# A DeltaNet and GELU kernel: chunk 0's masked Gram products taken from the plain Gram matrix, another home for chunk 2's Gram matrix, and a new order of the early work

## The chip, the cores and the metric

The kernel runs on one core of a Trainium2 chip. The metric is device time in microseconds; the median of several runs is compared. Beside the runs there is one profiled execution, whose trace shows every instruction on the engines PE (matrix unit; its weight loads are PEld), DVE (vector), ACT (scalar), POOL (GpSimd) and SP (here only a queue for DMA issues). ACT and POOL can issue DMAs too.

## The reference

Each of 4 x 8 heads runs a delta rule over 768 steps with a 48 x 48 state; the results, 3072 tokens of 384 numbers, go through a GELU network of width 2048.

```python
k_n = k / (np.linalg.norm(k, axis=-1, keepdims=True) + 1e-06)
state = np.zeros((B, H, D, D), dtype=np.float32)
for t in range(S):
    kt, vt, bt = (k_n[:, :, t].copy(), v[:, :, t].copy(), beta[:, :, t, None].copy())
    y[:, :, t] = np.einsum('bhd,bhde->bhe', q[:, :, t], state)
    v_old = np.einsum('bhde,bhd->bhe', state, kt)
    state = state + bt[:, :, :, None] * np.einsum('bhd,bhe->bhde', kt, vt - v_old)
x = y.transpose(0, 2, 1, 3).reshape(B * S, H * D)
h = x @ w_in
out = 0.5 * h * (1.0 + np.tanh(c * (h + 0.044715 * h * h * h))) @ w_out
```

## The kernel before

The sequence is cut into 12 chunks of 64 steps. A chunk c has two units, u = 2c and 2c + 1, each with 16 of the 32 heads; two heads share the 128 partitions. Within a chunk the delta rule is solved by the inverse of a triangular 64 x 64 matrix per head, built from 8 x 8 leaves upward; then the state is carried on and the chunk's 256 tokens go through the network. Every operation has a name with its chunk or unit behind the dot:

- Loads: k, q, v with chunk and quarter (k5.10 is a quarter of chunk 5's keys), beta, and w1, w2 (the weights, by POOL's queue). A chunk's k, q and v go to one of three buffers.
- Norms of the keys, per chunk (0a and 0b for the halves of chunk 0): sq (square), sum, pow (root), eps, inv.
- prep, per unit: kn (normalized keys), qb and vb (copies to bf16), knc, qbc, vbc (the same for both units of a chunk in one instruction); Tk, Tq or T (transposes on PE) and their copies kTk, kTq, kT; GD, GQ or G (Gram matrices of keys with keys and with queries), the copy dn of the first, wq (the second under its mask; wqa and wqb do it in two steps).
- leaf, per chunk: F gathers the leaves of dn, lp scales them, L spreads them, and x0, xm1 to xm6, xa1 to xa6 solve them step by step on DVE; xb ends it.
- scale, per unit: xe spreads xb to the block matrix zt (xec does both units at once); KZ multiplies the keys by zt, kz copies that, with the sign turned, to the third part of kT; GM forms the scaled Gram products from it (32 matmuls); lw writes them, under a mask, into the unit's lw buffer.
- invert, per unit: X10 and X11 put the leaves into the matrix bd, A4, rt4, B4, bde40 and bde41 join them to 32 x 32, A5, rt5, B5, be50 and be51 to 64 x 64.
- chain, per chunk: V, K, R (right hand side), U, Un (solution), S, Sn (new state), Q, O, On (output), X, xT (its transpose; turnx by DMA later).
- mlp, per chunk: up0 to up15 (3 matmuls each of 256 columns), gelu0 to gelu3, down00 to down13 (4 matmuls each of 384 columns), Z0, Z1, out.

Constants are made at the start (tmpl, ident, rows, blk, own, sel, unit, mlw, muq, two, low, pads, bdz, triwq, trilw, ladj). tabS and tabG are tiny activations that load ACT's tables for the square root and for the GELU. A fill is one matmul of 128 x 128 zeros by 128 x 512 zeros whose result nobody reads.

The order of all this is written out by hand in one list, ORDER (line 17 on). A word such as xe.1:d puts xe.1 on DVE (a, g, s: ACT, POOL, SP); a word with @4 is PE work that takes PSUM banks from bank 4 on. Each engine runs its words strictly in the order of the list. Flow.order (L152) finds from the list who must wait for whom, for data and for PSUM banks, and emit (L190) writes the semaphores.

## Time and profile before

| | us |
|---|---|
| median of 3 runs | 255.19 |
| the 3 runs | 253.28, 255.19, 255.27 |
| profiled execution, first to last instruction (its span; no other time of it is given) | 254.7 |
| PE busy | 226.0 (89%) |
| DVE busy | 185.8 (73%) |
| ACT busy | 157.4 (62%) |
| POOL busy | 130.1 (51%) |

A row of a timeline gives start and length in us, the engine, the line of the kernel, the operation, out<-in with the tile's names, shapes and a count; in brackets stands the idle time ahead of it and who ended it. A row of a grouping gives busy us and the mean ns of one, then the idle time ahead. Shares of busy time are averages over stages with different limits, so the windows matter more than this table.

### The profile page before, as it was taken

To read this page: it belongs to the slowest core of one execution; us is meant where nothing else is said; L and a number is where in the kernel's file an instruction comes from. 1 tells how busy PE (TensorE), PEld (TensorE's weight loads), DVE (VectorE), ACT (ScalarE), POOL (GpSimd) and SP (SyncE) were. 2 spreads that over 40 slices of the span, in tenths; PEclk is the share of its full clock that TensorE was granted. 3 is DMA by queue.
4 is the path that set the end of the run, shared out by engine and by line. 5 is a ranking of instruction groups with operands and counts; after the bars stand their busy time and mean duration, and the time that the engine had idled before them with its cause. 6 is when DMAs were issued, how large, how long until landed. Compare 5 with 4: busy or idle time off the path is not lost.

```text
span 254.7 us, 12256 instructions
## 1 busy us (share of the span) xinstructions
PE 226.0 (89%) x5500; PEld 178.3 (70%) x5502; DVE 185.8 (73%) x445; ACT 157.4 (62%) x244; POOL 130.1 (51%) x159
## 2 busy tenths in 40 slices
...
GB/s 103 165 144 118 184 162 95 165 127 117 128 130 105 112 126 124 135 165 147 119 146 167 100 36 131 147 153 130 56 93 167 62 49 4 33 68 64 3 93 62
DMA packets 104532, 28.25 MB, mean 111 GB/s; under 512 B 98592, under 2 KB 103712, under 8 KB 104480
## 3 DMA queue, kind: packets, MB, share of 16 engines
...
q8 instruction: 43, 0.70, 1.2%
q10 hardware_dynamic: 2400, 0.54, 1.1%
...
HBM read 20.64 MB, written 4.72 MB: 100 GB/s over the span
## 4 chain that ended last, share of the span: by engine, by line
PE 73%; DVE 15%; ACT 4%; DMA 2%; ACTq 2%; issue 2%; SPq 1%; POOL 0%
PE ps L835 24%; PE ps L824 22%; PE ps L692 5%; PE ps L620 3%; PE ps L752 3%; PE ps L773 2%; DMA vraw<-in_v_dram 2%; PE ps L697 2%; PE ps L564 2%; DVE lw L623 2%; DVE xl L658 2%; PE ps L633 2%; PE ps L759 2%; DVE ps L655 2%; PE ps L609 1%
## 5 line engine op out<-in xcount | busy, mean ns | idle before, releaser
L824 PE MATMUL ps<-xT,W 128*128 128x256 bf16 x576 | 76.8, 277 | 0.4 <-DVE xl L658 0.4
L835 PE MATMUL ps<-W,gT 128*128 128x384 bf16 x384 | 72.7, 326 | 0.0
L828 ACT ACTIVATE gT<-ps 128x1024 bf16<-128x1024 f32 x48 | 48.4, 1022 | 26.4 <-PE ps L824 25.8
L824 PEld LDWEIGHTS ps<-xT,W 128*128 128x128 bf16 x576 | 52.2, 99 | 9.3 <-DVE xl L658 0.5
L835 PEld LDWEIGHTS ps<-W,gT 128*128 128x128 bf16 x384 | 34.0, 97 | 18.2
L682 POOL TENSOR_SCALAR_AFFINE_SELECT bd<-lw 64x512 bf16<-64x512 bf16 x34 | 22.6, 667 | 37.7 <-DVE lw L623 28.6
L704 DVE TENSOR_TENSOR rl<-ps,two 128x384 bf16<-128x384 f32 (+1 forms) x48 | 22.9, 484 | 9.7 <-PE ps L692 9.5
L623 DVE CAST_PREDICATED lw<-mlw,ps 128x832 bf16<-128x832 uint16 x24 | 24.3, 1018 | 6.8 <-PE ps L620 6.5
L499 POOL TENSOR_TENSOR nrm<-nrm,half 128x16 f32<-128x16 f32 x9 | 26.6, 2956 | 2.8 <-DVE nrm L497 2.7
L343 ACT ACTIVATE bd<-ps 32x256 bf16<-32x256 f32 (+1 forms) x40 | 16.8, 428 | 8.2 <-PE ps L692 4.4
L692 PEld LDWEIGHTS ps<-lw,bd 128*128 128x128 bf16 x384 | 15.5, 98 | 4.2 <-POOL bd L682 1.2
L692 PE MATMUL ps<-lw,bd 128*128 128x32 bf16 (+1 forms) x384 | 17.2, 183 | 1.2 <-POOL bd L682 1.1
L658 DVE TENSOR_TENSOR xl<-ps,xl 128x96 bf16<-128x96 f32 (+4 forms) x72 | 16.0, 228 | 2.0
L655 DVE TENSOR_TENSOR ps<-ps,xl 128x64 f32<-128x64 f32 (+5 forms) x72 | 15.6, 221 | 2.0 <-PE ps L649 0.5
L343 ACT ACTIVATE ob<-ps 128x384 f32<-128x384 f32 x17 | 8.3, 490 | 14.0 <-PE ps L835 14.0
L722 POOL COPY bd<-xi 64x256 f32<-64x256 f32 x20 | 8.0, 401 | 16.4 <-ACT xi L343 8.5
L540 PE MATMUL ps<-ident,tok 128*128 128x128 bf16 x80 | 7.8, 246 | 8.1 <-POOL tok L531 3.8
L531 POOL TENSOR_TENSOR tok<-kraw,nrm 128x384 bf16<-128x384 f32 x9 | 8.5, 945 | 12.7 <-DVE bsb L349 5.6
L349 ACT ACTIVATE kT<-ps 128x512 bf16<-128x512 f32 x18 | 10.4, 596 | 6.4 <-PE ps L609 6.4
L343 ACT ACTIVATE dn<-ps 128x512 bf16<-128x512 f32 x18 | 10.4, 593 | 5.3 <-PE ps L564 5.3
L620 PE MATMUL ps<-kT 48*64 48x56 bf16 (+1 forms) x768 | 11.1, 196 | 2.8 <-ACT kT L349 1.4
L599 POOL TENSOR_TENSOR zt<-xb,blk 128x2048 bf16<-128x2048 bf16 x3 | 10.9, 3642 | 4.1 <-DVE xb L669 3.9
(132 smaller groups left out, 428.3 us busy)
## 6 DMA issues: line engine op xcount, KB each, us to landing
...
```

The lines of the kernel that those rows point to most:

```text
L343: return e.activation(out, in_, ACT.Copy) if e is nc.scalar else e.tensor_copy(out, in_)
L499: if e is nc.scalar else e.tensor_tensor(nr[:, 1, hx], nr[:, 0, hx], half[:, hx], ALU.pow), reads=[nrn, "half"] + ["one"] * (c < ROOTS),
L620: ins = e.matmul(P(ps("GM"))[hf(a), o_ + c0:o_ + c1], kT[s][r, y, g, hf(a)], kT[s][r, z, g, C * a + c0:C * a + c1])
L623: A(("dve",), op("lw"), lambda e, P: e.copy_predicated(lw[m][:, :, 0:LW - LB], mlw[:, :, :].rearrange("p w t -> p (w t)")[:, 16:16 + LW - ...
L655: A(("dve",), f"xm{m}.{c}", lambda e, P, m=m, w=w, part=part: e.tensor_tensor(part(P), P(f"L.{c}")[:, off[m]:off[m] + 2 * H * w].rearrange ...
L658: A(("dve",), f"xa{m}.{c}", lambda e, P, m=m, part=part: e.tensor_tensor(xl[y][:, :, m + 1:LB], part(P), xl[y][:, :, m + 1:LB], ALU.add), ...
L682: A(("pool", "dve"), op(f"X1{a}"), lambda e, P, src=lw[m][hf(a), :, LW - C:LW], dst=bd[b_][hf(a), :, hf(a)], a=a: e.affine_select(out=dst, ...
L692: ins = e.matmul(P(name)[:, C * h + c0:C * h + c1], bd[b_][:, h, :], rhs[:, h, :])
L704: A(("dve",), op(f"rt{i}"), lambda e, P, i=i, c0=c0, c1=c1, r_=r_: e.tensor_tensor(r_[:, 0:H, c0:c1], P(ps(f"A{i}")).rearrange("p (h t) -> ...
L824: ins = e.matmul(P(ph)[:, 256 * f:256 * f + 256].rearrange("p (x t) -> p x t", x=2), W1[:, j, 128 * (i + f):128 * (i + f) + 128], x_[:, :, ...
L828: A(("act",), f"gelu{i // 4}.{c}", lambda e, P, i=i, ph=ph: e.activation(g_[:, i:i + 4, :], P(ph).rearrange("p (f t) -> p f t", f=4), ACT. ...
L835: ins = e.matmul(P(po)[:, 0:DM], g_[:, f, 128 * b:128 * b + 128], W2[:, f, :], start=(f == 0), stop=(f == FC - 1))
```

## The change

The scaled Gram products are sums over the leaf index of entries that dn already holds: for chunk 0 GM is now formed from dn and zt directly (direct, 32 matmuls), and KZ.0, KZ.1, kz.0 and kz.1 go. The signs are kept by copying betaC0 without the minus and by putting it into R.0. dn of the even chunks stood in one buffer; chunk 2's now stands in the first quarter of gT2, a buffer that is first needed for chunk 2's GELU, and gelu0.2 waits for its readers. Loads and outputs may stand on ACT's queue too, and the count on a DMA's semaphore follows the list instead of the queues.

```diff
...
+        gram_of = [(dn[c % 2], c % 2) if c != 2 else (gT[2][:, 0:4, :].rearrange("p f (h t) -> p (f h) t", t=C), 2) for c in range(NC)]
...
-                    A(EV, f"betaC{i}", lambda e, P, i=i, d0=d0, d1=d1, w=w: neg(
+                    A(EV, f"betaC{i}", lambda e, P, i=i, d0=d0, d1=d1, w=w: (neg if i else copy)(
...
-                            A(("sp", "act") if c == 0 and n == "k" else SP, f"{n}{c}" + ("" if x is None else f"x{x}") + f".{a}{y}",
+                            A(("sp", "act"), f"{n}{c}" + ("" if x is None else f"x{x}") + f".{a}{y}",
...
-            d_, dnn = dn[c % 2][:, H * x:H * x + H, :], f"dn{c % 2}{x}"
+            d_, dnn = gram_of[c][0][:, H * x:H * x + H, :], f"dn{gram_of[c][1]}{x}"
...
-            def keys(e, P):
-                for g in range(4):
-                    for p, a in quad:
-                        ins = e.matmul(P(ps("KZ"))[hf(p), 512 * a + C * g:512 * a + C * g + C], tok[s][hf(a), 0, 2 * g + p, :], zt[m][hf(a), 4 * p + g, hf(a)])
-                return ins
-            A(PE, op("KZ"), keys, reads=[n("tok0"), f"zt{m}"], alloc=(ps("KZ"), 2), mode="t", mm=16)
-            A(EV, op("kz"), lambda e, P: neg(e, kT[s][:, 2, :, :].rearrange("p g (a t) -> p a g t", a=2), P(ps("KZ")).rearrange("p (a r) -> p a r", a=2)[:, :, 0:4 * C].rearrange("p a (g t) -> p a g t", g=4)),
-              frees=[ps("KZ")], writes=[n("kTz")])
-
...
-            A(PE, op("GM"), gram, reads=[n("kTk"), n("kTz")], alloc=(ps("GM"), 2), mode="t", mm=32)
+            def direct(e, P):
+                for g in range(4):
+                    for p in range(2):
+                        h, o_ = 4 * p + g, 512 * p + 2 * C * g
+                        for a in range(2):
+                            e.matmul(P(ps("GM"))[hf(a), o_ + LW - C:o_ + LW - LB], zt[m][hf(a), h, hf(a)], d_[hf(a), h, 0:C - LB])
+                        for a in range(2):
+                            ins = e.matmul(P(ps("GM"))[hf(a), o_:o_ + C - 16], d_[hf(a), h, :], zt[m][hf(a), h, C * a + 16:C * a + C])
+                return ins
+            if c < 1:
+                d_, dnn = gram_of[c][0][:, H * x:H * x + H, :], f"dn{gram_of[c][1]}{x}"
+                A(PE, op("GM"), direct, reads=[dnn, f"zt{m}"], alloc=(ps("GM"), 2), mode="t", mm=32)
+            else:
+                def keys(e, P):
+                    for g in range(4):
+                        for p, a in quad:
+                            ins = e.matmul(P(ps("KZ"))[hf(p), 512 * a + C * g:512 * a + C * g + C], tok[s][hf(a), 0, 2 * g + p, :], zt[m][hf(a), 4 * p + g, hf(a)])
+                    return ins
+                A(PE, op("KZ"), keys, reads=[n("tok0"), f"zt{m}"], alloc=(ps("KZ"), 2), mode="t", mm=16)
+                A(EV, op("kz"), lambda e, P: neg(e, kT[s][:, 2, :, :].rearrange("p g (a t) -> p a g t", a=2), P(ps("KZ")).rearrange("p (a r) -> p a r", a=2)[:, :, 0:4 * C].rearrange("p a (g t) -> p a g t", g=4)),
+                  frees=[ps("KZ")], writes=[n("kTz")])
+
+                A(PE, op("GM"), gram, reads=[n("kTk"), n("kTz")], alloc=(ps("GM"), 2), mode="t", mm=32)
...
-                    ins = e.matmul(P(f"F.{c}")[:, 0:2 * H * (LB - 1)], sel[:, i, :], dn[y][:, :, LB * i + 1:LB * i + LB], start=(i == 0), stop=(i == NLB - 1))
-                return ins
-            A(PE, f"F.{c}", fold, reads=["sel", f"dn{y}0", f"dn{y}1"], alloc=(f"F.{c}", 1), mode="m", mm=NLB)
+                    ins = e.matmul(P(f"F.{c}")[:, 0:2 * H * (LB - 1)], sel[:, i, :], gram_of[c][0][:, :, LB * i + 1:LB * i + LB], start=(i == 0), stop=(i == NLB - 1))
+                return ins
+            A(PE, f"F.{c}", fold, reads=["sel"] + [f"dn{gram_of[c][1]}{x}" for x in range(2)], alloc=(f"F.{c}", 1), mode="m", mm=NLB)
...
-            A(EV, op("R"), lambda e, P: copy(e, rb[:, :, :, :, :].rearrange("p y x g d -> p y (x g d)"), banks(P(ps("K")))), frees=[ps("K")], writes=[rbn])
+            A(EV, op("R"), lambda e, P: (neg if first else copy)(e, rb[:, :, :, :, :].rearrange("p y x g d -> p y (x g d)"), banks(P(ps("K")))), frees=[ps("K")], writes=[rbn])
...
-                  reads=["one"], frees=[ph], writes=[f"{gn}.{i // 4}"])
+                  reads=["one"], frees=[ph], writes=[f"{gn}.{i // 4}"] + ([f"dn2{x}" for x in range(2)] if c == 2 and not i else []))
...
-                        A(SP, f"out{a}{a}.{c}", lambda e, P, a=a, o_=o_: e.dma_start(
+                        A(("sp", "act"), f"out{a}{a}.{c}", lambda e, P, a=a, o_=o_: e.dma_start(
```

In emit, the loop that counts each operation's tag runs over self.queue instead of over the engines' queues one after the other; nothing else is changed there.

The list is rewritten up to about chunk 3's leaves and unit 11; behind that the engines' orders are the same, with other PSUM banks. These are the engines' orders of the early part, from the start to the first up-projections (words without banks).

```
before
PE: betaT1 betaT0 Tk.1 Tk.2 Tk.3 Tq.1 GD.3 Tq.0 GD.2 GD.1 betaS1 Tk.0 F.1 GQ.1 GD.0 L.1 GQ.0 F.0 betaS0 betaS3 L.0 T.5 Tq.3 T.4 betaS2 Tq.2 G.5 G.4
  KZ.1 GM.1 KZ.0 F.2 L.2 GM.0 KZ.2 KZ.3 GM.3 A4.1 A4.0 B4.1 GQ.2 GM.2 B4.0 V.0 A4.3 A5.1 GQ.3 A5.0 B4.3 B5.1 B5.0 fill115 A4.2 U.0 KZ.4 O.0 A5.3 S.0
  GM.4 X.0 B4.2 fill85 KZ.5 up4.0 up0.0 up1.0 up2.0 up12.0 up3.0 A5.2 up13.0
DVE: bdz3 bdz5 pad0 pad5 trilw0 bdz4 mmlw identf sel unit mmuq betaN101 sum.0b betaN100 eps.0b inv.0b betaN001 sum.1 betaN011 betaN110 pad3 inv.1
  triwq1 betaN010 low1 kn.2 kn.3 kTk.2 betaN111 kTk.1 kTq.1 sum.0a betaH1 eps.0a inv.0a betaN000 betaL1 betaH0 sum.2 first0 kTq.0 kTk.0 lp.1 betaL0
  x0.1 two inv.2 wz xm1.1 wq.0 xa1.1 xm2.1 xa2.1 lp.0 xm3.1 ladj5.1 ladj4.1 x0.0 xm1.0 xa1.0 xa3.1 xm2.0 xa2.0 xm4.1 xm3.0 xa3.0 xa4.1 xm5.1 xm4.0
  xa4.0 xa5.1 xm5.0 xm6.1 xa6.1 xa5.0 kTq.3 xm6.0 xa6.0 xb.0 xe.1 xe.0 wq.4 xec.1 lw.1 lp.2 bdz1 x0.2 lw.0 xm1.2 xa1.2 lw.3 rt4.1 xm2.2 xa2.2 xm3.2
  xa3.2 rt4.0 xm4.2 wq.2 lw.2 xa4.2 xm5.2 rt4.3 rt5.1 rt5.0 xa5.2 xm6.2 xa6.2 be50.1 wq.3 be51.0 xe.4 bde41.3 rt4.2 sum.3 rt5.3 xe.5 lw.4 sum.4 kz.5
  X10.4 qbc.3 rt5.2 eps.3 inv.3 knc.3 lw.5
ACT: k0x1.10 k0x1.00 beta10 k0x1.11 beta00 k0x0.00 trilw1 k0x0.10 tabS sq.0b k0x0.11 pow.0b sq.1 k0x0.01 ladj4.0 pow.1 qb.1 sq.0a kTk.3 pow.0a sq.2
  dn.3 dn.2 dn.1 pow.2 dn.0 qbc.2 betaC0 triwq2 wqa.1 kT.5 betaC1 kT.4 betaC2 kTq.2 dn.4 kz.1 dn.5 ladj5.0 wqa.5 betaC3 kz.0 kz.3 kz.2 vb.0 bde40.1
  bde41.1 bde40.0 bde41.0 R.0 bde40.3 be50.0 be51.1 sq.3 Un.0 kz.4 On.0 sq.4 Sn.0 xT.0 bde40.2 bde41.2 tabG gelu0.0 gelu3.0 gelu1.0 be51.3 be50.2
  gelu2.0 be51.2 R.1
POOL: tmplz tmpl0 tmpl1 blk1 one pad2 ident ident2 bdz0 blk2 blk3 half own triwq4 triwq0 mln0 bdz2 pad4 mwp0 rowz mln1 pad1 kn.1 muq0 muq1 eps.1 qb.0
  rows1 rpad0 kn.0 low2 eps.2 trilw2 knc.2 w1.0 first1 qb.3 trilw3 qb.2 xb.1 triwq5 w1.1 mwp1 X10.1 X11.1 rpad1 X11.0 X10.0 X11.3 vb.1 triwq3 X10.3
  wqb.1 X11.2 X10.2 xb.2 w2.0 w2.1 X11.4 pow.3 X11.5 vbc.1 pow.4 bdc40.5 bdc41.5 eps.4 wqb.5
```
```
after
PE: betaT1 betaT0 Tk.3 Tk.2 Tk.1 GD.3 GD.2 betaS1 Tq.0 Tq.1 Tk.0 F.1 GD.0 L.1 fill136 GD.1 GQ.0 fill111 betaS0 F.0 T.5 L.0 betaS2 fill132 GQ.1 fill104
  fill92 T.4 Tq.2 fill27 G.4 G.5 GM.1 Tq.3 fill25 fill69 KZ.3 F.2 fill73 GM.0 L.2 fill84 A4.1 fill4 fill29 fill45 GM.3 B4.1 KZ.2 A4.0 fill40 GQ.2
  fill137 GQ.3 fill133 B4.0 GM.2 fill97 A5.1 fill19 fill129 fill83 betaS3 A5.0 B5.1 A4.3 B5.0 fill74 V.0 B4.3 A4.2 fill77 fill114 fill47 U.0 fill116
  fill57 KZ.4 fill23 B4.2 O.0 A5.3 X.0 S.0 GM.4 B5.3 up0.0 up1.0 up2.0 up3.0 up4.0 up5.0 up6.0 up7.0 KZ.5 up8.0 up9.0 up12.0 up10.0 up13.0
DVE: pad5 wz tmplz bdz4 half identf low1 rpad1 triwq4 blk1 mmlw sum.0b unit pad3 trilw2 pad2 sq.1 betaN011 sum.1 eps.0b inv.0b eps.1 inv.1 kn.3
  ladj5.0 pad1 sum.0a betaN110 own kTk.3 betaN010 betaN111 betaN101 betaN100 betaH1 eps.0a mmuq betaL1 sel triwq1 inv.0a kTk.1 dn.3 betaN000 bdz3
  sum.2 kTk.0 lp.1 betaN001 betaH0 x0.1 eps.2 betaL0 xm1.1 ladj4.0 qbc.2 inv.2 xa1.1 xm2.1 xa2.1 wq.0 xm3.1 lp.0 xa3.1 xm4.1 x0.0 xm1.0 xa4.1 xa1.0
  xm5.1 xm2.0 xa2.0 xa5.1 xm3.0 betaC0 xa3.0 xm6.1 xm4.0 xa6.1 xa4.0 xm5.0 xa5.0 xm6.0 xa6.0 xec.1 xb.0 xe.1 dn.4 lw.1 kTq.3 lp.2 wq.4 lw.0 x0.2 xm1.2
  xa1.2 rt4.1 xm2.2 lw.3 xa2.2 xm3.2 xa3.2 rt4.0 xm4.2 xa4.2 wq.2 lw.2 xm5.2 wq.3 xa5.2 rt5.1 xm6.2 rt5.0 xa6.2 X10.2 rt4.3 be51.0 be51.1 xec.2 rt4.2
  bde41.3 sum.3 rt5.3 kz.4 Sn.0 be50.3 lw.4 X10.4 X11.4 eps.3 sum.4 inv.3 knc.3 rt5.2 lw.5 X10.5 R.1 rt4.5 rt4.4
ACT: k0x0.00 beta10 k0x1.10 k0x1.11 k0x1.00 q0.01 k1.11 sq.0b k0x0.11 q0.11 q2.11 tabS k2.00 pow.0b pow.1 sq.0a q1.00 kTk.2 pow.0a q2.00 q1.01 sq.2
  dn.2 kTq.1 trilw3 pow.2 kTq.0 ladj4.1 betaC1 dn.0 dn.1 kT.5 two qbc.1 wqa.1 kT.4 kTq.2 dn.5 triwq3 wqa.5 tabG kz.3 betaC2 bde40.1 bde41.1 kz.2 k4.01
  bde40.0 ladj5.1 bde41.0 q3.00 sq.3 be50.1 be50.0 R.0 bde40.3 betaC3 Un.0 On.0 bde40.2 xT.0 gelu0.0 be51.3 bde41.2 gelu1.0 kz.5 k5.11 qbc.3
POOL: ident rowz ident2 tmpl0 bdz0 tmpl1 pad0 trilw1 one low2 pad4 blk2 rows1 mln0 triwq0 first1 kn.1 blk3 trilw0 kn.2 mwp0 qbc.0 triwq5 kn.0 muq0
  muq1 w1.0 rpad0 mln1 kn.5 kn.4 bdz1 mwp1 bdz5 w1.1 first0 xb.1 triwq2 xe.0 X10.1 X11.1 X11.0 X10.0 vb.0 wqb.1 X10.3 vb.1 bdz2 X11.2 X11.3 xb.2 w2.0
  vbc.1 sq.4 w2.1 pow.3 X11.5 wqb.5
```

In SP's and ACT's queues, the first loads are ordered anew, and these loads go from SP's queue to ACT's: q0.01, k1.11, q0.11, q2.11, k2.00, q1.00, q2.00, q1.01, k4.01, q3.00, k5.11, q4.01, q5.10, q5.01, q6.00 and k7.00; beta00, k0x0.10 and k0x0.01 go the other way. All outputs stay on SP's queue except those of the last chunk that were on ACT's already. Further on, dn.9, dn.11, kz.6, be51.4 and the bde of units 4 and 5 go to DVE, kz.5, kT.6 and Z0.0 to ACT.

198 lines of the change are left out of this document (99 added, 99 removed).

## The prediction

> **What bounds the kernel now.** I read the busy time by stages first, cut where the granted clock changes (columns: window, its length, busy us with instruction count of PE, PEld, DVE, ACT, POOL, then clock, DMA share, GB/s).
>
> ```profile
> span 254.7 us, 12256 instructions
> 26.10:29.50 3.40, 2.15 (x60) 1.68 (x60) 3.13 (x19) 2.24 (x5) 1.16 (x4) 1.00 1.07 188
> 29.50:32.90 3.40, 1.45 (x72) 1.12 (x72) 3.40 (x5) 2.77 (x7) 0.76 (x2) 1.00 1.31 201
> 32.90:36.30 3.40, 1.89 (x102) 1.73 (x102) 2.82 (x7) 1.60 (x5) 1.45 (x3) 0.50 1.12 191
> 36.30:39.70 3.40, 2.34 (x90) 2.02 (x83) 3.03 (x9) 1.16 (x4) 2.86 (x6) 0.50 0.35 63
> 39.70:43.10 3.40, 3.39 (x83) 3.13 (x84) 3.29 (x10) 2.64 (x5) 2.99 (x4) 0.50 0.60 97
> 43.10:46.50 3.40, 1.92 (x81) 1.59 (x79) 3.34 (x8) 3.02 (x6) 2.19 (x3) 0.99 0.92 144
> 46.50:49.90 3.40, 2.99 (x118) 2.67 (x104) 3.40 (x5) 3.33 (x6) 0.54 (x1) 0.51 1.21 176
> 49.90:53.30 3.40, 3.40 (x24) 2.41 (x17) 1.65 (x4) 2.27 (x4) 3.07 (x2) 0.50 1.32 205
> 26.10:46.50 20.40, 13.14 (x466) 11.28 (x467) 19.00 (x54) 13.44 (x25) 11.40 (x20) 0.75 0.89 147
> 53.30:250.00 196.70, 194.02 (x4692) 152.02 (x4690) 141.62 (x323) 124.14 (x186) 98.06 (x95) 1.00 0.59 102
> ```
>
> The reader is to see two kernels in one. From 53.3 to 250 us PE is busy 194.0 of 196.7 us and sets the pace: work that reaches it earlier ends earlier. From 26.1 to 46.5 us DVE is busy 19.0 of 20.4 us, while PE has 7.3 us of gaps. And the clock is 0.50 in 32.9 to 43.1 and in 46.5 to 53.3, five windows of one length: it fell behind the windows in which PE was busy 1.45 and 1.92 us of 3.40, held behind 2.15, and rose only behind 3.39 and 3.40.
>
> The chain that ended last gives the price of a matmul at either clock (start, length, count).
>
> ```profile
> 50.01 3.74 PE ps L824 x18
> 241.07 4.91 PE ps L824 x45
> 245.98 5.21 PE ps L835 x32
> ```
>
> A matmul of 256 columns takes 3.74/18 = 208 ns in the slow stretch and 4.91/45 = 109 ns later; one of 384 columns 5.21/32 = 163 ns. So two things decide: when chunk 0's up-projection reaches PE (now up4.0 at 50.0), and the clock that it meets (now full at 53.3).
>
> **The change, part by part.** *Clock.* The new order has 27 fill matmuls instead of 2, all between L.1 and B4.2, ahead of up0.0. No fill's matmul record is in the trace; from the two rows above I estimate 163 + 54 = 217 ns for its 512 columns at full clock, twice that at half: 5.9 us in all, against the 7.3 us of gaps. If the clock stays up, the 3.3 us from 50.0 to 53.3 shrink to 3.3 x 109/208 = 1.75. **Gain 1.55 us.** The other bound is nothing, if the clock falls all the same; I take the gain, since with the fills the windows from 33 us on come to 2.7 us and more of 3.4 by the times below, nearer to those that held than to those that fell.
>
> *DVE up to U.0.* Rows of the first 55 us, by operation (the dn row is from later, dn being ACT's until then).
>
> ```profile
> 13.06 1.96 DVE L531 TENSOR_TENSOR tok<-kraw,nrm 128x384 bf16<-128x384 f32 x1
> 14.95 0.54 DVE L531 TENSOR_TENSOR tok<-kraw,nrm 128x384 bf16<-128x384 f32 x1
> 23.92 0.94 DVE L418 TENSOR_SCALAR rl<-tmpl 128x256 bf16<-128x256 bf16 x2
> L343 DVE COPY kT<-ps 128x512 bf16<-128x512 bf16 x6 | 2.3, 416 | 0.3 <-PE ps L540 0.2
> L602 DVE TENSOR_TENSOR zt<-xb,blk 128x1024 bf16<-128x1024 bf16 x4 | 2.7, 702 | 0.1
> L421 DVE MEMSET bd<- 128x512 f32 x4 | 1.9, 485 | 1.1 <-PEq L889 1.0
> L343 DVE CAST bd<-ps 32x256 bf16<-32x256 f32 x2 | 0.8, 410 | 0.0
> L343 DVE CAST dn<-ps x6: 627/692/692, 66.0 to 201.3; 128x512 bf16<-128x512 f32 x6
> L524 DVE TENSOR_TENSOR tok<-kraw,nrm 128x768 bf16<-128x768 f32 x1 | 1.0, 959 | 0.0
> L343 DVE CAST tok<-qraw 128x768 bf16<-128x768 f32 x1 | 0.5, 545 | 0.0
> L343 DVE COPY wq<-tmpl 128x512 bf16<-128x512 bf16 x1 | 0.5, 510 | 0.0
> L571 DVE CAST_PREDICATED wq<-muq,ps 128x512 bf16<-128x512 uint16 x4 | 2.7, 674 | 0.0
> L623 DVE CAST_PREDICATED lw<-mlw,ps 128x832 bf16<-128x832 uint16 x5 | 5.1, 1017 | 0.8 <-PE ps L620 0.8
> L704 DVE TENSOR_TENSOR rl<-ps,two 128x384 bf16<-128x384 f32 x4 | 2.2, 550 | 0.0
> ```
>
> DVE loses kn.2 (1.96), kTk.2, kTq.1, kTq.0 (3 x 0.42), xe.0 (0.70), bdz1, bdz5 (2 x 0.49), ladj4.1, ladj5.1 (0.94 the pair), be50.1 (0.41) and an estimated 0.9 of small things and trilw0: 7.2 us. It gets sq.1 (no such row: between ACT's 0.84 and the 0.96 of a two-input product of that size; I take 0.96), dn.3, dn.4 (2 x 0.69), qbc.2 (0.55), triwq4, trilw2 (2 x 0.51), ladj4.0, ladj5.0 (0.94), X10.2 and be51.1 (0.41 each) and an estimated 1.2 of memsets, eps and betaC0: 6.9 us. DVE is exchanged, not relieved.
>
> ```profile
> 9.00 0.55 DVE L497 TENSOR_REDUCE nrm<-sq 128x8 f32<-128x384 f32 x1 [1.40 <-ACT sq L495]
> 22.14 0.24 DVE L655 TENSOR_TENSOR ps<-ps,xl 128x96 f32<-128x96 f32 x1
> 29.13 0.29 DVE L669 TENSOR_TENSOR xb<-xl,bc 128x128 bf16<-128x128 bf16 x1
> ```
>
> At the head DVE waits for ACT's first square and starts at 9.00. In the new order only loads stand ahead of that square on ACT, so it runs about 1 us sooner; but the square root's table load comes behind three more DMA issues, and sel, triwq1 and the beta copies move behind it on DVE. Laid end to end, xm1.1 comes at 22.6 (22.14 now), and xb.0, behind xec.1 (two zt halves, 1.2 us, for chunk 1), ends at 31.1 instead of 29.4.
>
> *Gram products of chunk 0.* KZ (16 matmuls), its copy kz on ACT, and GM (32) become one GM of 32.
>
> ```profile
> 31.23 0.44 PE L620 MATMUL ps<-kT 48*64 48x56 bf16 x32 [0.71 <-ACT kT L349]
> 34.79 1.02 DVE L623 CAST_PREDICATED lw<-mlw,ps 128x832 bf16<-128x832 uint16 x1 [0.46 <-PE ps L620]
> 34.34 1.46 POOL L682 TENSOR_SCALAR_AFFINE_SELECT bd<-lw 64x512 bf16<-64x512 bf16 x2 [4.02 <-DVE xl L640]
> L602 POOL TENSOR_TENSOR zt<-xb,blk x5: 1909/1913/1916, 133.3 to 194.0; 128x1024 bf16<-128x1024 bf16 x5
> 38.93 0.55 DVE L704 TENSOR_TENSOR rl<-ps,two 128x384 bf16<-128x384 f32 x1
> ```
>
> GM.1, now at 31.23, starts behind xe.1 at 31.8: the steps saved pay for xec.1, no more. xe.0 goes to POOL (1.91 instead of 0.70) and ends at 33.0; lw.0 stands on DVE behind dn.4, lw.1, kTq.3, lp.2 and wq.4 until 34.3, so that hides POOL's slowness; uncovered it would cost 1.2 us. The direct products alternate between two parts of PE instead of four: between 0.44 and 0.88 us each, hidden behind dn.4 and wq.4. POOL's 4.02 us wait is for bdz1, which stood behind lp.2 on DVE; it moves to early POOL, so X10.1 follows lw.1 at 33.1 and A4.1 comes by 34.5. DVE takes that up again: x0.2, xm1.2, xa1.2, rt4.1 (36.4), xm2.2, lw.3, three leaf steps, rt4.0 (38.2 to 38.7; now 38.93), two leaf steps, wq.2, lw.2 (40.6), wq.3 and two, rt5.1, rt5.0 (42.5), X10.2, rt4.3 (43.5), be51.0, be51.1: 44.4.
>
> Chunk 2's Gram room: with dn0 shared, dn.4 would wait for the direct GM.0 (33.4) and hold lw.1 behind it by over 1 us; in gT2 it waits for nothing. gelu0.2 gets a wait on readers that are long done.
>
> ```profile
> 44.70 0.57 PE L773 MATMUL ps<-rs,bd 128*128 128x48 bf16 x16 [0.85 <-DVE bd L343]
> 48.83 0.81 ACT L343 ACTIVATE xT<-ps 128x768 bf16<-128x768 bf16 x1
> 50.71 1.28 ACT L859 ACT_TABLE_LOAD   x1
> ```
>
> *From U.0 to up0.0.* V.0, B4.3, A4.2 and three fills stand ahead of U.0: 45.0 (44.70 now). Then Un.0 behind betaC3 on ACT 45.75 to 46.55, O.0, On.0 47.0 to 47.8 (ACT copies of this width take 0.81), X.0, and xT.0 behind bde40.2, 48.4 to 49.2 (48.83 now); S.0, GM.4 and B5.3 go first on PE: up0.0 at 49.5. up4.0 now starts at 50.0 with KZ.5 done and B5.3 to do, here the reverse. **Gain 0.5 us.** The gelu table (1.28) is loaded before 34 us; now it hides behind PE's slow up matmuls: worth nothing by itself.
>
> *Loads on ACT.* Eight loads of SP's now stand among ACT's copies behind 37 us, about 0.6 us of issue each; the readers of their buffers end earlier, so I count none as waiting; if one does, everything behind it on ACT waits too.
>
> **Sum.** 0.5 + 1.55 = 2.05 us, kept to the end since PE has only 2.7 us of gaps behind 53.3. 254.7 - 2.05 = 252.65; the median shown, 255.19, lies 0.5 above that span, so **253.1**. About 1% (2.55 us) is what a measurement of this kernel can tell from no change.
>
> **A rule and a row.** kn.2 took 1.96 us on DVE, its twin 0.54.
>
> ```profile
> 12.63 2.05 POOL L382 TENSOR_SCALAR_AFFINE_SELECT rows<-rows 128x1024 bf16<-128x1024 bf16 x1
> ```
>
> kn.2 ended at 15.02, 0.34 behind POOL's 14.68: DVE was held. The Trainium skill (GPSIMD Engine Reference, section 1, Specifications) says that GpSimd shares its SBUF interfaces with VectorE and contends with DVE instructions of two SBUF inputs; by that rule, the trace agrees. It speaks against xe.0 on POOL beside xe.1 on DVE: rival 2.
>
> **Rivals.** 1. *The clock falls again* (0.15). Between T.4 (25.7) and GM.1 the new order has only Tq.2, G.4, G.5 and a fill, some 1.4 of 3.4 us, as little as the window behind which it fell now. If it is not back by 46 us, the 1.55 go: 254.7.
> 2. *POOL holds DVE* (0.12). If xe.1 is held until xe.0 ends, lw.1 and all behind it on DVE come 1.2 us late, once or, with kn.4, kn.5 and qbc.0 in the head, twice: 254.3 to 255.5.
> 3. *Slower: DVE late at lw.5* (0.08). kz.4, Sn.0 and R.1 (0.7 to 1 us each) are new on DVE ahead of lw.5 and rt4.5. I get lw.5 done at 56.5, and PE, in order, wants A4.5 at 57.6. From 1 us of lateness each microsecond stops PE; at 3 us the gain is gone, at 5 to 6 it is 256 to 257, at 7 over 257.7. Against it: DVE is busy only 1.65 of 3.40 us in 49.9 to 53.3 now.
> 4. *Better* (0.2). The head keeps its full microsecond and the 1.4 us for which kn.2 was held do not come back: U.0 at 43, 251 to 252.
>
> That the Gram part does nothing is in the sum already: its steps are paid out to xec.1 and POOL.
>
> **How the numbers follow.** The forecast, 2.05 give or take 1, has 0.45. Faster by over 1% (below 252.64) is rival 4 and the better third of the forecast, 0.2 + 0.17 = 0.37. Slower by over 1% (above 257.7) is rival 3's far end and what I don't see: 0.06. Within 1%: 0.57. The range takes in rival 4 to 250.9, rivals 1 and 2, and rival 3 to 256.0.
>
> **What would show it.** Right: clock 1.0 from 33 to 53 us, up0.0 between 49 and 50 with matmuls of 109 ns from the first; DVE full up to U.0 at 45; A4.1 near 34.5. Wrong: a window at 0.50 behind 46; xe.1 over 1 us long; PE idle ahead of A4.5; U.0 off 45 by more than a microsecond.

## The result, and the profile after

| | time, us (median of its runs) | profiled span, us |
|---|---|---|
| before | 254.3 | 254.7 |
| after | 261.48 (261.18 to 261.72) | 259.8 |

The changed kernel takes 1.0272 times as long, 95% interval [1.0227, 1.0317]: about 7 us slower, where 2 us less were forecast. A note on the two spans: in nineteen later profiled executions, where both are known, the time lies 1.7 to 1.9 us above the span (2.4 in one). By that the execution of before that was profiled took about 256.5 us (an estimate), 2 us more than the median, which is why the spans differ by only 5.1 us.

The busy time of the changed kernel by stages, cut where its clock changes (window, length, busy us with count of PE, PEld, DVE, ACT, POOL, then clock, DMA share, GB/s):

```profile
30.60:34.00 3.40, 1.20 (x37) 0.92 (x38) 3.05 (x6) 3.09 (x5) 2.73 (x2) 1.00 1.12 200
34.00:37.50 3.50, 3.28 (x65) 2.46 (x66) 1.49 (x3) 1.09 (x2) 1.00 (x2) 0.51 1.10 157
37.50:47.50 10.00, 8.41 (x244) 5.96 (x247) 9.39 (x27) 5.55 (x11) 7.69 (x12) 1.00 0.42 76
47.50:51.10 3.60, 1.75 (x46) 1.10 (x47) 3.60 (x3) 1.51 (x3) 2.51 (x3) 1.00 1.13 146
51.10:57.90 6.80, 5.85 (x133) 4.60 (x131) 5.21 (x10) 2.09 (x3) 2.94 (x1) 0.50 1.02 159
57.90:250.00 192.10, 189.54 (x4670) 148.25 (x4668) 143.73 (x324) 123.20 (x186) 97.92 (x92) 1.00 0.58 102
```

The clock was to stay at 1.00 from 33 to 53 us. It fell twice, behind a window in which PE was busy 1.20 of 3.40 us and behind one of 1.75 of 3.60, and the full clock comes at 57.9 us instead of 53.3. Behind that the stage has PE busy 189.5 of 192.1 us, as before. Most of the loss is made ahead of 60 us: chunk 0's first gelu starts at 58.13 us, 4.4 us later than before. The lag then grows to 6.9 us at gelu1.4 and is 5.1 us at the end. It shows in three places.

**First place: chunk 0's Gram products.** The timeline of the changed kernel, from xe.0 on POOL to lw.0 on DVE:

```profile
31.08 2.41 POOL L603 TENSOR_TENSOR zt<-xb,blk 128x1024 bf16<-128x1024 bf16 x1 [1.60 <-DVE xb L683]
32.51 1.02 DVE L637 CAST_PREDICATED lw<-mlw,ps 128x832 bf16<-128x832 uint16 x1 [0.18 <-PE ps L621]
33.59 0.11 PEld L427 LDWEIGHTS ps<-wz 128*128 128x128 bf16 x2 [0.97 <-DVE lw L637]
34.49 0.93 PE L647 MATMUL ps<-gT,sel 128*128 128x112 bf16 x8
35.46 0.28 DVE L651 TENSOR_TENSOR lp<-ps,bsb 128x112 bf16<-128x112 f32 x1 [1.60 <-PE ps L647]
35.79 0.13 PEld L619 LDWEIGHTS ps<-dn,zt 64*64 64x64 bf16 x2 [0.51 <-DVE lp L651]
36.88 1.02 DVE L637 CAST_PREDICATED lw<-mlw,ps 128x832 bf16<-128x832 uint16 x1 [0.55 <-PE ps L621]
```

The last operand of GM.0 (xe.0, the first row) is there at 33.49, and GM.0 starts at 35.79. In between PE works its list in order: a fill (L427) that needs the PSUM bank of GM.1 and so waits for lw.1 (the second row), then KZ.3, then F.2 (L647), whose bank GM.0 needs next, so that GM.0 waits for lp.2 (35.46). lw.0 ends at 37.9 instead of 35.8 before, and U.0 comes at 47.50 instead of 44.70: 2.8 us.

**Second place: xec.2, O.0 and up0.0.** The same timeline from POOL's vbc.1 to the first up matmuls:

```profile
46.87 0.84 POOL L344 CAST vb<-vraw 128x768 bf16<-128x768 f32 x1
47.11 3.12 DVE L600 TENSOR_TENSOR zt<-xb,blk 128x2048 bf16<-128x2048 bf16 x1
47.50 0.56 PE L787 MATMUL ps<-rs,bd 128*128 128x48 bf16 x16
47.66 1.47 POOL L497 TENSOR_TENSOR sq<-kraw 128x768 f32<-128x768 f32 x1
50.28 0.32 PE L630 MATMUL ps<-zt,tok 64*64 64x64 bf16 x16 [1.79 <-DVE zt L600]
51.09 0.63 PE L809 MATMUL ps<-us,wq 64*64 64x48 bf16 x32
54.33 0.25 PE L796 MATMUL ps<-us,tok 64*64 64x48 bf16 x4 [0.37 <-issue]
55.37 1.04 PE L838 MATMUL ps<-xT,W 128*128 128x256 bf16 x4
```

An operation of this shape (xec.1) took 1.21 us in the kernel before:

```profile
31.33 1.21 DVE L599 TENSOR_TENSOR zt<-xb,blk 128x2048 bf16<-128x2048 bf16 x1
```

xec.2 took 3.12; it ran from the middle of vbc.1 to 1.10 us past the end of chunk 4's squares (sq.4), both on POOL. PE's list has KZ.4 (L630), which reads xec.2 and waited 1.79 us for it, and B4.2 ahead of O.0 (L809), whose own operand Un.0 was there at 49.01. up0.0 starts at 55.37; the first up matmuls before started at 50.01.

**Third place: SP's queue.** Chunk 3's query copy (qbc.3) and the transpose turn.7 that waits for it, before:

```profile
51.00 0.55 DVE L343 CAST tok<-qraw 128x768 bf16<-128x768 f32 x1
55.79 2.46 SPq L553 DMA_TRANSPOSE kT<-tok  x1
```

and after:

```profile
61.54 0.85 ACT L344 ACTIVATE tok<-qraw 128x768 bf16<-128x768 f32 x1
62.42 2.09 SPq L554 DMA_TRANSPOSE kT<-tok  x1
```

The copy is now on ACT behind two gelus of chunk 0, so turn.7 is issued 6.6 us later, and with it all loads that stand behind it on SP.

### The profile page after: what moved, and what is told of

It reads as the page before. It is cut to its first block, busy times and chain, and to the rows that moved or that the text cites. A ratio compares the mean times of both kernels' runs of the same rounds, so it can differ in the third digit from the quotient of the medians.

```text
span 259.8 us, 12216 instructions
## 1 busy us (share of the span) xinstructions
PE 231.0 (89%) x5487; PEld 178.7 (69%) x5495; DVE 188.7 (73%) x453; ACT 154.1 (59%) x238; POOL 132.4 (51%) x152
## 4 chain that ended last, share of the span: by engine, by line
PE 72%; DVE 8%; ACT 6%; DMA 5%; SPq 3%; issue 2%; ACTq 2%; POOL 0%; DVEq 0%
PE ps L849 23%; PE ps L838 20%; PE ps L706 5%; DMA kraw<-in_k_dram 3%; SPq L473 3%; PE ps L565 2%; PE ps L766 2%; PE ps L711 2%; PE ps L612 2%; PE ps L647 2%; DMA kT<-tok 2%; DVE zt L600 2%; PE ps L787 2%; PE ps L773 2%; PE ps L796 2%
## 5 line engine op out<-in xcount | busy, mean ns | idle before, releaser
L838 PE MATMUL ps<-xT,W 128*128 128x256 bf16 x576 | 75.9, 276 | 0.1
L696 POOL TENSOR_SCALAR_AFFINE_SELECT bd<-lw 64x512 bf16<-64x512 bf16 x32 | 21.3, 670 | 36.8 <-DVE lw L637 31.4
L344 ACT ACTIVATE bd<-ps 32x256 bf16<-32x256 f32 (+1 forms) x38 | 15.9, 425 | 12.2 <-PE ps L706 6.6
L669 DVE TENSOR_TENSOR ps<-ps,xl 128x96 f32<-128x96 f32 (+4 forms) x72 | 15.8, 222 | 2.3 <-PE ps L663 0.6
L672 DVE TENSOR_TENSOR xl<-ps,xl 128x96 bf16<-128x96 f32 (+3 forms) x72 | 16.1, 227 | 1.8
L736 POOL COPY bd<-xi 64x256 f32<-64x256 f32 x18 | 7.2, 401 | 16.5 <-ACT xi L344 9.0
L603 POOL TENSOR_TENSOR zt<-xb,blk 128x1024 bf16<-128x1024 bf16 x6 | 11.9, 1996 | 5.5 <-DVE xb L683 5.4
L344 DVE CAST bd<-ps 32x256 bf16<-32x256 f32 (+1 forms) x23 | 10.0, 442 | 6.0 <-ACT bd L344 3.2
L498 DVE TENSOR_REDUCE nrm<-sq 128x16 f32<-128x768 f32 (+1 forms) x13 | 11.4, 876 | 4.0 <-ACT sq L496 3.9
L565 PE MATMUL ps<-kT 48*64 48x128 bf16 (+1 forms) x448 | 10.4, 221 | 3.0 <-ACT kT L344 0.9
```

Source lines behind the costliest of these rows:

```text
L344: return e.activation(out, in_, ACT.Copy) if e is nc.scalar else e.tensor_copy(out, in_)
L565: ins = e.matmul(o, kT[s][r, y, g, hf(a)], kT[s][r, z, g, hf(a)])
L669: A(("dve",), f"xm{m}.{c}", lambda e, P, m=m, w=w, part=part: e.tensor_tensor(part(P), P(f"L.{c}")[:, off[m]:off[m] + 2 * H * w].rearrange ...
L672: A(("dve",), f"xa{m}.{c}", lambda e, P, m=m, part=part: e.tensor_tensor(xl[y][:, :, m + 1:LB], part(P), xl[y][:, :, m + 1:LB], ALU.add), ...
L696: A(("pool", "dve"), op(f"X1{a}"), lambda e, P, src=lw[m][hf(a), :, LW - C:LW], dst=bd[b_][hf(a), :, hf(a)], a=a: e.affine_select(out=dst, ...
L838: ins = e.matmul(P(ph)[:, 256 * f:256 * f + 256].rearrange("p (x t) -> p x t", x=2), W1[:, j, 128 * (i + f):128 * (i + f) + 128], x_[:, :, ...
```

## The experiments

All ratios are to the kernel before, run on the same chip. "Pads" are small matmuls of 16 columns whose results nobody reads.

**One edit each on the changed kernel.** The diffs are words of the order.

a_nofill:
```
- fill136@2 ... fill23@2        (all 27)
```


> The changed kernel without its 27 fill matmuls; nothing else differs. Theory (PE's order and PSUM banks make chunk 0's Gram products late): without the fills, PE reaches KZ.3 and F.2 as soon as lw.1 frees the bank at 33.5 us instead of 33.8 and later, GM.0 still waits for lp.2 by the bank that it shares with F.2, and comes at 34.8 to 35.4 us instead of 35.79; U.0 ends its wait at 46.5 to 47.2 instead of 47.50. The clock falls over more windows: the first squares stay at half speed for one window longer (8.4 instead of 7.0 us for the first). Sum of the two: time within 1.5 us of the changed kernel's 261.5, so 260 to 263. Rival (the fills themselves cost the time, by standing in PE's order ahead of work that is due): 256 to 258. Rival (the fills are what keeps the changed kernel from being worse): 263 to 265, with granted clock at 0.5 from 30 to 45 us.

Measured: 264.93 us, 1.0424 [1.0356, 1.0491]. GM.0 came at 34.61, a little ahead of what the theory had, and U.0 at 47.20, within it. The first square on ACT ran at 6.82 us, no later than with the fills (6.99). The clock has to be read with care here. A row of the windows, and U.0 in the timeline:

```profile
46.50:49.90 3.40, 1.58 (x43) 1.31 (x40) 3.37 (x3) 2.33 (x4) 2.81 (x3) 1.00 1.00 119
47.20 0.80 PE L785 MATMUL ps<-rs,bd 128*128 128x48 bf16 x16 [0.24 <-ACT rs L348]
```

The clock column says 1.00, but U.0's sixteen matmuls took 0.80 us, against 0.56 at 1.00 in the changed kernel (second place above), and the up matmuls start 0.21 us apart until 55.4 and 0.11 us apart from there on. The trace has no record of the clock ahead of 55.4 us, and the column shows 1.00 where it has none. So PE ran at half speed up to 55.4 us: the fills did keep the clock up in the changed kernel, though not throughout. Even so gelu0.0 came 1.8 us earlier than with them (56.33 for 58.13). The time was lost behind that, in waits of PE from 45 to 130 us that the view puts down to "issue" (in total, times, longest):

```profile
PE ps L794 <- issue: 1.3, 1, 1.3
PE ps L628 <- issue: 1.2, 1, 1.2
PE ps L764 <- issue: 1.1, 1, 1.1
PE ps L807 <- issue: 0.6, 1, 0.6
```

These come to 4.2 us, against 0.5 in the changed kernel. Time and clock are those of the last rival, but the loss behind 56 us is not the clock's; what such waits are comes out of the experiments on the Gram part below.

a_o0:
```
- KZ.4@6 fill23@2 ... B4.2@4 ... O.0@0
+ O.0@0 KZ.4@6 fill23@2 ... B4.2@4
```


> The changed kernel with one word moved: chunk 0's last product of the early part, O.0, stands ahead of KZ.4, fill23 and B4.2 in PE's order. Theory (O.0 stands in PE's order behind KZ.4, which waits for xec.2 on DVE): O.0 starts when Un.0 lands, at 49.1 to 49.4 instead of 51.09 us, up0.0 at 53.4 to 53.8 instead of 55.37, time 259.5 to 260.0. Rival (Un.0 and On.0 are late themselves, since DVE is behind by 2 us at the same place, so that O.0's place costs nothing): On.0 still at 51.5 to 51.8, time 261.0 to 261.7.

Measured: 261.54 us, 1.0264 [1.0209, 1.032]. O.0 ran at 48.83 and On.0 at 49.33, 2.3 and 2.4 us earlier, but X.0 still stood behind B4.2 (51.39), and then PE stopped for 1.07 us inside S.0. up0.0 came at 54.65, and the time did not move.

a_sq4:
```
- sq.4:g                    (ahead of O.0)
+ xT.0:a sq.4:a
```


> The changed kernel with one operation on another engine: chunk 4's squares (sq.4) on ACT behind xT.0 instead of on POOL. Theory (POOL's vbc.1 and sq.4 hold DVE's xec.2, which reads two tiles of SBUF): xec.2 takes 1.2 to 2.0 us instead of 3.12, so KZ.4 and O.0 come 1.2 to 1.9 us earlier, time 259.6 to 260.3. Rival (xec.2 is long for a reason of its own, its source tiles or its queue): still 3.0 to 3.2 us, time 261.2 to 261.8. Rival (sq.4 on ACT now delays what ACT does next, S.0's gelu and the copies behind it): xec.2 short, but the time 261 to 263.

Measured: 260.93 us, 1.0255 [1.0196, 1.0313]. Timeline of this kernel, xec.2 and the end of S.0:

```profile
46.41 1.69 DVE L600 TENSOR_TENSOR zt<-xb,blk 128x2048 bf16<-128x2048 bf16 x1
53.76 0.25 PE L796 MATMUL ps<-us,tok 64*64 64x48 bf16 x4 [2.58 <-issue]
```

xec.2 fell from 3.12 to 1.69 us, so POOL had held it. What that gained was lost four matmuls from the end of S.0: PE stopped for 2.58 us there, and the view names no engine that it waited for ("issue").

a_bank:
```
- fill25@4 fill69@2 ... F.2@4 fill73@5 ... betaC2:a
+ F.2@1          (betaC2:a, which empties bank 1, behind kTq.2:a)
```


> The changed kernel with GM.0's PSUM bank kept free: three fills that use bank 4 or 5 ahead of it (fill25, fill69, fill73) are dropped, F.2 writes bank 1 instead of bank 4, and the copy that empties bank 1 (betaC2) moves behind kTq.2 on ACT. Theory (GM.0 is late by the banks that it and the matmuls ahead of it wait for, not by its data): GM.0 at 33.5 to 34.2 us instead of 35.79, lw.0 ends 34.6 to 35.3 instead of 36.88, rt4.0 38.5 to 39.5 instead of 40.88, U.0 45.2 to 46.2 instead of 47.50; the wait at xec.2 stays, so the time falls by 1.0 to 2.0 us to 259.5 to 260.5. Rival (the data are late: xe.0 on POOL ends 33.49 and POOL's and DVE's queues behind it set the next steps): lw.0 earlier, but rt4.0 and U.0 within 0.4 us of the changed kernel, time 261.0 to 261.7.

Measured: 260.22 us, 1.0248 [1.0172, 1.0324]. Timeline: GM.0, lw.0, U.0.

```profile
33.99 0.21 PE L619 MATMUL ps<-dn,zt 64*64 64x56 bf16 x2
34.91 1.02 DVE L637 CAST_PREDICATED lw<-mlw,ps 128x832 bf16<-128x832 uint16 x1
45.89 0.56 PE L787 MATMUL ps<-rs,bd 128*128 128x48 bf16 x16
```

The banks were the cause at the first place: GM.0 came 1.8 us earlier and U.0 1.6 us earlier. The median time is 1.3 us less, but the four runs spread from 259.06 to 262.69 us and the interval overlaps that of the changed kernel, so a gain in time is not shown.

b_sp:
```
- k5.11:a ... turn.7:s ... v2.00:s v2.01:s q4.11:s k5.00:s q4.01:a v2.10:s v2.11:s k5.01:s q4.00:s q4.10:s q5.00:s q5.10:a ... q5.01:a
+ v2.00:s ... q5.01:s (all fourteen on SP) turn.7:s
```


> The changed kernel with SP's queue freed: the transpose turn.7, which waits for chunk 3's query copy on ACT, stands behind fourteen loads of chunks 4 and 5 and v2 instead of ahead of them (four of these come back from ACT to SP). Theory (two limits side by side: the late start of up0.0, and the loads that queue behind turn.7 on SP): up0.0 and the first gelu stay where they are (58.1 us, 4.4 later than before), but the lag to the kernel before no longer grows from 3.7 us at gelu2.0 to 6.9 at gelu1.4; it stays at 4 to 5, time 258.5 to 260. Rival (the loads come early enough in any case; the later lag comes from elsewhere): lag 6 to 7 at gelu1.4, time 261 to 262.

Measured: 260.86 us, 1.0307 [1.0259, 1.0356]. The lag to the kernel before was 3.4 us at gelu2.0 and 5.3 at gelu1.4: it still grew, by 1.9 us instead of 3.2. The time is not clearly apart from the changed kernel's 1.0272 [1.0227, 1.0317], so nothing shows that SP's queue costs the changed kernel time. Neither text is borne out in full.

b_bank_sp (a_bank and b_sp together):

> Both edits together: the banks of GM.0 freed as in a_bank, and SP's queue freed as in b_sp. Theory (two limits side by side, each of which hides most of what the other's removal gains): gelu2.0 lags by 0.7 us as in a_bank, and the lag stays under 2 us to gelu1.4 instead of growing to 4.9; time 254.5 to 257, so the two together bring 4 to 6 us, though each alone brings 1 to 2.5. Rival (the loss behind 60 us has another cause): lag 4 to 5 at gelu1.4 as in a_bank, time 259 to 260.5.

Measured: 259.51 us, 1.0229 [1.0185, 1.0273], in the rival's range. The lag was 1.7 us at gelu2.0 and 4.2 at gelu1.4. Timeline:

```profile
45.96 2.40 POOL L497 TENSOR_TENSOR sq<-kraw 128x768 f32<-128x768 f32 x1
52.45 0.18 PE L796 MATMUL ps<-us,tok 64*64 64x48 bf16 x1 [2.31 <-issue]
```

Here DVE's xec.2 got through in 1.69 us and POOL's sq.4 was the one that took long, 2.40 instead of 1.47 us. And again PE stopped inside S.0, now one matmul from its end, for 2.31 us.

**Parts of the change alone, on the kernel before.**

b_qbc:
```
- qbc.3:d                   (ahead of gelu0.0)
+ gelu1.0:a qbc.3:a turn.7:s
```


> The kernel before with one step of the change alone: chunk 3's query copy qbc.3 goes from DVE (51.0 us) to ACT behind gelu1.0, as in the changed kernel; turn.7 on SP, and all loads behind it, wait for that. Theory (SP's queue is a limit by itself): turn.7 at 60.5 to 61.5 us instead of 55.8, the loads behind it 5 us later, PE idle for 2 to 4 us between 70 and 90 us, time 256.0 to 258.5. Rival (the loads have 5 us to spare in the kernel before): 253.5 to 255.

Measured: 256.79 us, 1.0133 [1.01, 1.0167]: 3.4 us slower, as the theory had it, by moving one copy of 0.55 us. turn.7 was issued at 58.24 (expected 60.5 to 61.5). The expected idle time of PE at 70 to 90 us was not found; the longest wait that the view names behind 56 us is 1.0 us, for a copy on ACT. So the price is shown, the path by which it reaches the end is not: the moved copy delays SP's loads, and it also takes 0.84 us of ACT between gelus, and the run does not part the two.

b_gram:
```
- KZ.1@4 kz.1:a   KZ.0@0 kz.0:a     (in the order of before; the program is that of the changed kernel)
```


> The change's first two parts alone: the changed kernel's program with the order of the kernel before, less the four steps that are gone (chunk 0's KZ and kz). Chunk 0's masked Gram products are made straight from the Gram matrix, chunk 2's Gram matrix lies in the activations' room. Theory (the Gram part is worth little either way, the order costs the time): GM.1 at 30.4 to 31.0 instead of 31.23 us, U.0 44.0 to 44.7, time 252.5 to 255. Rival (the direct products or the shared room cost the time by themselves): U.0 at 46 or later, time over 257.

Measured: 260.13 us, 1.0277 [1.0238, 1.0317]. This was the surprise: the Gram part alone is as slow as the whole change, though U.0 came at 45.01, only 0.3 us late. The timeline ahead of X.0, in which On.0 makes the operand xo and X.0 transposes it:

```profile
46.99 0.81 ACT L343 ACTIVATE xo<-ps 128x768 bf16<-128x768 f32 x1
50.08 0.39 PE L820 MATMUL ps<-ident,xo 128*128 128x128 bf16 x2 [2.11 <-ACT st L343]
```

X.0 reads nothing but xo (there at 47.80) and the identity, and its bank is the one that On.0 emptied; the copy st that the view names is not among its inputs. PE had nothing to wait for and stood still for 2.11 us. What did happen in that time is a packet of the instruction queue (DMA parts of a half microsecond, 47.5 to 48.0):

```profile
q8 instruction: 1, 0.02, 12.2%
```

The page of the kernel before lists 43 such packets with 0.70 MB, so 16 KB each; PE has 5500 matmuls and 5502 weight loads there, so 256 of them to a packet. c_before_pad below, with 11196 in all instead of 11002, has 44. I read this as PE's instructions being brought in by DMA while the program runs. X.0 started 2.4 us behind the start of that packet, and the stops of 2.58 and 2.31 us above ended 2.4 us behind the start of one. Waits put down to "issue", 45 to 130 us, in b_gram (total, times, longest):

```profile
PE ps L629 <- issue: 1.6, 2, 1.3
PE ps L795 <- issue: 0.8, 1, 0.8
PE ps L808 <- issue: 0.8, 1, 0.8
PE ps L765 <- issue: 0.4, 1, 0.4
```

These 3.6 us and the 2.11 ahead of X.0 make 5.7 of the 6.7 us by which b_gram is slower than the kernel before on that chip (253.42 us). In the kernel before there is only:

```profile
PE ps L795 <- issue: 0.2, 1, 0.2
```

The Gram part has 32 matmuls and 32 weight loads fewer. That moves the end of every later block of 256 by 64 instructions of work. The Trainium skill (Runtime: NRT & Kernel Launch, section Instruction fetch mechanics) says that an engine's instructions come in 16 KiB blocks of 256, fetched while the block before is worked off, and that the cost of crossing into the next is mostly hidden. The packets here agree in size. That the cost is hidden fits the kernel before, with 0.2 us of such waits, but not b_gram with its 5.7 us, as the next two runs show.

**The place at which code blocks end, and nothing else.**

c_gram_pad, c_before_pad:
```
+ for _ in range(32): e.matmul(P("pad0x")[:, 0:16], ident[:, 0:128], ident[:, 0:16])    # b_gram and one such group
+ the same with range(48), two groups                                                    # the kernel before and two such groups
```


> The Gram part alone (as in b_gram) with 32 small matmuls of 16 columns added at about 14 us, where PE is idle; nobody reads what they compute. They put back the 64 PE instructions (32 weight loads, 32 matmuls) by which b_gram is shorter than the kernel before, so that the 16 KB blocks in which PE's code comes in end at the same steps as in the kernel before. Theory (b_gram lost its time to PE waiting for code: 2.1 us ahead of X.0, and 2 to 3 us more in such waits up to 130 us): X.0 follows On.0 within 0.3 us, up0.0 at 50.0 to 50.6, the waits that end 2.2 to 2.8 us behind the start of a code packet sum to under 2 us instead of 4.8 to 5.6, time 253.0 to 255.5. Rival (the Gram products themselves cost the time): X.0's wait stays, time 259 to 261.

> The kernel before with nothing changed but 96 small matmuls of 16 columns, two groups of 48 between 12 and 17 us, whose results nobody reads: 192 PE instructions more, which is the same place in a block of 256 as the 64 fewer of b_gram. Theory (the place at which PE's code blocks end decides over microseconds): a wait of 1 to 2.3 us between O.0 and up0.0 and others up to 130 us, time 256 to 260. Rival (the place of the blocks is worth nothing, or PE waits for code only when something else is late): 253 to 255; the pads themselves cost at most 0.7 us if PE's idle time there doesn't take them up.

Measured: c_gram_pad 254.64 us, 1.0018 [0.9993, 1.0044]; c_before_pad 259.93 us, 1.0221 [1.0166, 1.0276]. The pads themselves cost nothing. Before, and then c_before_pad with its second group and the step behind it:

```profile
15.08 1.50 PE L540 MATMUL ps<-ident,tok 128*128 128x128 bf16 x12 [3.26 <-DVE tok L531]
```

```profile
11.61 1.47 PE L427 MATMUL ps<-ident 128*128 128x16 bf16 x48
15.08 1.50 PE L546 MATMUL ps<-ident,tok 128*128 128x128 bf16 x12 [2.00 <-DVE tok L537]
49.65 0.82 PE L813 MATMUL ps<-ident,xo 128*128 128x128 bf16 x6 [1.62 <-ACT st L343]
```

The twelve transposes start at 15.08 in both, and 35 us later X.0 has the stop of b_gram (1.62 us). The waits put down to "issue", 45 to 130 us, are back in c_before_pad:

```profile
PE ps L615 <- issue: 1.2, 1, 1.2
PE ps L788 <- issue: 0.8, 1, 0.8
PE ps L758 <- issue: 0.5, 1, 0.5
```

and gone in c_gram_pad:

```profile
PE ps L814 <- issue: 0.3, 1, 0.3
```

So 64 instructions whose results nobody reads bring the Gram part from 1.0277 to 1.0018, and 192 make the kernel before 5.5 us slower. The Gram products themselves are worth nothing either way.

The stops also stand where blocks of 256 would put them. The number of PE's weight loads and matmuls that the trace records ahead of a stop is 1453 in b_gram (X.0) and a_o0 (S.0), 1454 in a_sq4 (S.0), 1456 in b_bank_sp (S.0), and 1710, which is 1454 and 256, in c_before_pad (X.0): the same place in a block, within three records, whatever step stands there. The clock is not the cause: executions of b_gram with a mean clock of 0.964 and 0.967 took 260.19 and 259.57 us, of c_gram_pad with 0.963 and 0.966 took 254.10 and 253.83.

c_gram_w2:
```
- xb.2:g ... w2.0:g ... w2.1:g ... X11.4:g      (b_gram)
+ w2.0:g X11.0:g ... X11.4:g w2.1:g
```


> The Gram part alone (as in b_gram) with the two 768 KB loads of the second weight matrix moved on POOL: the first from 44.1 to about 36 us, the second from 45 to about 50 us; PE's instructions are those of b_gram. Theory (the code packet ahead of X.0 comes late because the weight load fills the DMA engines at 44 to 57 us): the packet starts 1 us or more earlier than 47.6, the wait ahead of X.0 is under 1 us instead of 2.1, time 257 to 259. Rival (the packet starts when PE gets near the end of its code, whatever else is moving): the wait stays 1.9 to 2.3 us, time 259.5 to 261.5.

Measured: 260.28 us, 1.0213 [1.0162, 1.0264], not clearly apart from b_gram. The loads went out at 36.10 and 51.10. The packet started at 48.2, no earlier than in b_gram; X.0's stop shrank to 1.33 us, but a new stop of 0.46 us came inside U.0. The time is the rival's, the stop lies between the two. Why a packet comes late is left open by this run.

**Is the changed kernel's loss the place of its blocks, too?** Its order with 32, 64 and 96 pads at 10 us:

> The changed kernel with 32 small matmuls of 16 columns added at about 10 us, where PE is idle; nobody reads their results. PE's code blocks end 64 instructions earlier in the work. Theory (the order costs the changed kernel its time: U.0 2.8 us late by PSUM banks, 1.8 us at xec.2, both without any wait for code): 258 to 263, whatever the place of the blocks. Rival (its loss is mostly the place of the blocks, as for the Gram part alone): one of the three places tried gives 253 to 256.

> The same with 64 small matmuls in two groups of 32: blocks end 128 instructions earlier in the work. Theory (order): 258 to 263. Rival (place of the blocks): 253 to 256 for one of the three.

> The same with 96 small matmuls in two groups of 48: 192 instructions. Theory (order): 258 to 263. Rival (place of the blocks): 253 to 256 for one of the three.

Measured: 261.27, 264.78 and 263.70 us (1.0291 [1.0248, 1.0334], 1.0418 [1.038, 1.0455], 1.0372 [1.0314, 1.043]). With its own 261.48 that makes four places, none under 261: the order itself costs, about 7 us against the better of the two places tried for the kernel before, 1 to 5 us against the worse.

**The clock term by itself.** d_fill is c_gram_pad with 15 of its 32 pads turned into fills of 512 columns:
```
+ F.2@3 fill0@0 ... fill6@0   KZ.3@0 fill7@2 fill8@2   fill9@5 fill10@5 A4.0@1   fill11@1 fill12@1 fill13@1 U.0@0   fill14@7 O.0@6
```


> The Gram part alone with PE's count of instructions put back, as in c_gram_pad, but 15 of its 32 extra matmuls are now fills of 512 columns in PE's gaps (7 behind F.2 at 31.5 us, 2 behind KZ.3, 2 ahead of A4.0, 3 ahead of U.0, 1 ahead of O.0), each in a PSUM bank that has been empty for a while. Theory (the clock falls behind windows of 3.4 us in which PE is idle for half and more; fills that wait for nothing keep it up): clock 1.00 from 33 to 53 us, up0.0 at 49 to 50.2 with matmuls of 109 ns from the first, gelu0.0 1.5 to 2.5 us earlier than in c_gram_pad, time 251.5 to 253.5. Rival (fills delay what stands behind them by as much as they bring): 254 to 256. Rival (the work behind 53 us has its own limit, by DVE or the loads, and takes up what comes early): gelu0.0 early by 1.5 us or more, but the time within 0.5 us of c_gram_pad's 254.6.

Measured: 254.42 us, 0.9996 [0.9969, 1.0023]. Stages and first up matmuls of d_fill:

```profile
46.50:49.90 3.40, 2.42 (x134) 2.05 (x135) 3.40 (x6) 3.25 (x6) 0.30 (x1) 1.00 1.18 164
49.90:53.30 3.40, 3.31 (x39) 2.82 (x43) 2.22 (x5) 3.28 (x6) 3.31 (x2) 1.00 1.29 190
```

```profile
49.99 2.14 PE L844 MATMUL ps<-xT,W 128*128 128x256 bf16 x18 [0.93 <-ACT xT L344]
```

(The first eighteen matmuls took 3.74 us before.) The clock is up from 34.4 us, and PE now waits 0.93 us for xT on ACT ahead of the up matmuls. gelu0.0 came only 0.4 us earlier than in c_gram_pad (52.58 against 52.99), which by the place of its windows had the clock back at 51.1 anyhow, and the time is the same: the last rival comes nearest. This is not one lucky execution: the mean clock of all twelve is 0.986 to 1.00, against 0.963 to 0.973 in the ten of c_gram_pad.

**The order mended.**

c_all (a_bank, a_o0, a_sq4, b_sp and w2.0, w2.1 behind X11.1):

> The changed kernel with all of the edits that were tried on it one by one (banks of GM.0 freed, O.0 ahead of KZ.4, sq.4 on ACT, SP's loads ahead of turn.7) and with both loads of the second weight matrix issued on POOL at 35 us instead of 46 and 49. Theory (late start of up0.0, loads behind turn.7, and code that comes late are all that sets it back): U.0 at 45.5 to 46.0, O.0 at 47.5 to 48.0, up0.0 at 50.0 to 51.0, time 253.0 to 256.0; each wait of PE for code that falls into it costs up to 2.3 us more. Rival (another limit, not yet named, holds it): 257.5 to 260.

Measured: 261.16 us, 1.0267 [1.0226, 1.0309]. U.0 came at 48.91, later than in the changed kernel: the weight load on POOL waited 1.38 us for a load and then took 1.82, and X11.0 and X10.0 waited behind it. The edit spoilt what it was to test.

> The changed kernel with the two edits of b_bank_sp (GM.0's banks freed; SP's loads ahead of turn.7), and 74 small matmuls at 10 to 15 us whose results nobody reads: PE's code blocks end 148 instructions earlier in the work, which by 256 is 108 later, so that the block that ended inside S.0 in b_bank_sp (PE waited 2.31 us for code there) ends among the first up matmuls. Theory (the order's loss is the banks and the queue, the rest of b_bank_sp's is that wait for code): no wait of that kind between U.0 and the first gelu, gelu0.0 at 53.5 to 54.5, time 254.5 to 257.5. Rival (waits for code only move elsewhere, or a further limit of the order holds): 258 to 261.

> The same with 32 small matmuls: the blocks end 64 instructions earlier than in b_bank_sp, which puts the end ahead of X.0, where the code still comes at about 52 us. Theory (the place of the block's end decides): the wait for code stays, 1.5 to 2.3 us ahead of X.0, time 258.5 to 260.5, so 2 to 4 us above e_pad74. Rival (the two times agree within 1 us): the place is not what decides.

Measured: e_pad74 263.32 us, 1.0367 [1.0294, 1.0441]; e_pad32 260.19 us, 1.0213 [1.015, 1.0276]. e_pad74 missed by 6 us: the block's end went in among the up matmuls as meant, PE stopped there for 1.53 us, and stops of 0.2 to 0.6 us followed. e_pad32 has the time that was expected for it but not the stop ahead of X.0, and it was to be 2 to 4 us slower than e_pad74 and is 3 us faster. In both POOL held xec.2 again, for 3.12 and 3.07 us. The place of the blocks seems to decide over 3 us here too, but where a stop falls was not to be worked out ahead of the run.

No version that was run beats the kernel before. c_gram_pad and d_fill equal it and beat the changed kernel by 7 us.

## Why the prediction was wrong, step by step

*DVE up to U.0* was right as far as it went: xm1.1 came at 22.61 (forecast 22.6), the end of xb.0 at 31.0 (31.1), GM.1 at 31.78 (31.8).

*Gram products of chunk 0* is the first step that failed. I timed GM.0 by its data and by DVE's list ("between 0.44 and 0.88 us each, hidden behind dn.4 and wq.4") and not by PE's list and its PSUM banks: a fill in GM.1's bank and F.2 in GM.0's. GM.0 came 2.4 us behind the 33.4 of the forecast and lw.0 2.6 behind, and U.0 2.5 behind (47.50 for 45.0). a_bank shows the cause and gives 1.6 us of it back at U.0. That xe.0 took 2.41 us on POOL and not 1.91 added 0.5 us ahead of that.

*From U.0 to up0.0* is the second: 4.5 us were forecast (45.0 to 49.5) and 7.9 came (47.50 to 55.37). It failed at a wait that the prediction does not have: xec.2 stands ahead of KZ.4, and KZ.4 and B4.2 ahead of O.0, so that PE waited 1.8 us. POOL's hold on DVE was rival 2, with the row and the rule for it, but I looked for it at xe.1 beside xe.0, which took 0.69 us and was not held (xe.0 was the longer one); it came at xec.2 beside vbc.1 and sq.4, for 1.9 us.

*Clock*, 1.55 us, mostly did not come, by the first two: a fill that waits for a bank leaves the gap that it was to fill, and the wait for xec.2 made the second gap. Between the two, from 37.5 to 47.5, PE was busy 2.9 us of each 3.4, as forecast, and the clock held. But the up matmuls still met half clock for 2.5 us (55.4 to 57.9) where they had met it for 3.3; by the two matmul prices of the prediction that is a gain of about 0.4 us, an estimate. Rival 1 had the mechanism, with the window of 1.4 us (it was 1.20). d_fill shows that fills in free banks keep the clock, and that the term was too large even so: 0.4 us at the first gelu against a kernel whose windows lie well, and nothing measurable in the time.

*Loads on ACT* were counted at nothing, and no run shows that they cost anything by themselves. Missed was the copy qbc.3 among them, behind which turn.7 and SP's loads stand. In the kernel before its move costs 1.3% (b_qbc); that it costs the changed kernel time is not shown, since b_sp, which frees the loads, is no faster. The rule to follow each moved step into each queue behind it was applied to the loads and not to what they wait for.

*Sum.* The base was off as well: a time lies 1.7 to 1.9 us above its span, not 0.5, so the profiled execution of before was a long one, and the forecast took the gain off it; with a fourth run the median of before is 254.32 us and not 255.19.

Rival 3 had the right sign and the wrong place: lw.5 was late (it began at 62.22 and was to be done at 56.5), and no wait of PE for it is among the named ones. Missing altogether was the place of PE's code blocks: up to 5.5 us for an order that is not changed at all. Against it every term of the sum was small, and a change that alters the count of PE's instructions (the Gram part by 64) moves it. In the changed kernel, though, it is not what was lost: its waits put down to "issue" come to 0.5 us from 45 to 130 us, and at three other places of its blocks (d_pad32 to d_pad96) no time is under 261.

Still open: up0.0's delay of 5.4 us (2.8 by U.0, 2.6 from U.0 on, of which PE's wait for xec.2 is 1.8) is as large as the 5.1 us between the two profiles. But the lag grows to 6.9 us at gelu1.4 before it falls to 5.1, and the median times differ by 2 us more than the profiles; neither has a cause that a run shows. Nor is the account closed by its repair: mending the named causes did not bring the order under 259.5. Also open is why a code packet starts late; the weight load that fills the DMA engines at 44 to 57 us was not shown to be the reason (c_gram_w2).
